# Attention with every score and value matmul on the two 64-row halves of the TensorE array

## The chip, the cores and the metric

The kernel runs on one core of a Trainium2 chip. The metric is device time in microseconds of one execution, the median of several. The profile is of one execution of its own, with times counted from the first instruction.

## The reference

A block of 2048 tokens (width 640) goes through a layer norm without weights, then through attention over a stored cache of keys and values and, beside it, through a gated hidden layer. The two are multiplied and added to the input.

```python
xn = _layernorm(x)                                     # x: 2048 x 640
q = (xn @ wq).reshape(B, Sq, 32, 192)                  # 32 heads, 192 wide
scores = einsum("bhqd,bhkd->bhqk", q, k_cache) * 192 ** -0.5
o = einsum("bhqk,bhkd->bhqd", softmax(scores), v_cache)  # 2048 keys a head
s = o.reshape(B, Sq, 32 * 192) @ wo                    # 6144 -> 640
h = silu(xn @ w1) * (xn @ w3)                          # 640 -> 1536
g = silu(h @ w2)
out = x + s * g
```

All inputs are bf16.

## The kernel before, in words

**Order of work.** After the layer norm of the first 512 tokens the kernel goes head by head (32), and in a head block by block of 512 queries (4, `qb`). Instructions wrapped in `pin` keep the order in which the program writes them on their engine, so the order on TensorE is the order of the Python calls. What is not pinned (some GpSimd copies, loads) is placed by the scheduler.

**Scores, transposed.** Keys lie transposed in SBUF, so that a score tile has 128 keys as rows and 512 queries as columns. The 192 values of a key are split: `KA` holds 128 of them on 128 partitions, `KB` the other 64. A 64-deep matmul fills half of the array's rows. Key tiles are therefore taken in pairs (`p` and `p + 8`, of 16): `KB` holds the last 64 values of the second half of the keys on partitions 64 to 127 and, by a GpSimd copy (line 101), those of the first half on partitions 0 to 63. Query values lie likewise in `qA` (128), `qF` (partitions 64 to 127) and `qD` (a copy on partitions 0 to 63, line 225). For one pair `scores` issues two full matmuls (line 293, into the two 512-column halves of a score tile `st2`) and then two 64-row matmuls, one on each half of the array (line 300), that add to the same places. One ScalarE exponential over 128 x 1024 (line 303) turns the pair into `pT2`, with a bias per head (`nb`) that bounds the scores from above.

**Values.** `pT2` is the stationary operand of the value matmuls (line 323): for both key tiles and each of the block's four tiles of 128 queries, 128 keys deep, with 193 columns. The last column of `vt` is one, so that the sum of the exponentials comes out beside the values. The four query tiles add up in two banks (`obank`, two tiles each) over all 16 key tiles. At the end of a block VectorE takes the reciprocal of the sum (line 339) and multiplies (line 340) into `ostage`, which is stored to DRAM after every second head (line 344).

**Batches.** `advance` takes two or three pairs at once (`uneven`, line 349; `even` with two in head 0): all their full score matmuls, all their 64-row ones, and then the value matmuls of the batch before. In the first batch of a block `between` stands ahead of the values: the projection of the next head's queries (`project_chunk`, lines 219 to 222, ten matmuls with 512 columns, cast by VectorE at lines 223 and 224), and in odd heads a piece of the hidden layer (`swiglu_chunk`) on ScalarE and GpSimd. Half of the columns of `wqB` are hidden-layer weights, so that a part of the hidden layer is projected on the way. VectorE also takes maxima of absolute queries and keys (lines 229 and 237), from which `finish_head` makes `nb`. In head 0 `block_bound` does that for each block, and transposes of the normalised tokens (`next_turn`) and the projections of heads 0 and 1 come between batches.

**Tiles in PSUM.** `ps_st` has three tiles of 1024 f32 (scores, projections, transposes), `ps_o` two of 512: 4096 f32 a partition.

**Loads.** `load_head(h + 2)` is called at the start of head `h`. On SyncE's queue it puts two DMA transposes of 2048 keys by 128 columns (lines 98 and 100) and the load of the values (line 103), and on GpSimd's queue the weights. Three heads of keys fit.

**Tail.** After the last head come 16 hidden-layer chunks (`ffn_hidden`, line 445; the first of them ahead of the last value matmuls), the hidden layer's output (`ffn_out`, line 496) and the product with `wo` (`output_tile`, line 480).

Of the kernel before, what the change touches and what calls it, by code (L numbers as in the profile page):

```python
# [8 lines left out]
ACT = mybir.ActivationFunctionType  # L9
ALU = mybir.AluOpType  # L10
# [19 lines left out]
def _kernel_impl(ctx, tc, A_x, A_k_cache, A_v_cache, A_wq, A_wo, B_w1, B_w3, B_w2, out):  # L30
# [21 lines left out]
    eps = 1e-5  # L52

# [40 lines left out]
    def load_head(h):  # L94
        kh = A_k_cache[0, h]
        vh = A_v_cache[0, h]
        KA = kvp.tile([P, SK], BF16, tag="KA")
        nc.sync.dma_start_transpose(out=KA[:], in_=kh[:, 0:P])
        KB = kvp.tile([P, SK], BF16, tag="KB")
        nc.sync.dma_start_transpose(out=KB[:], in_=kh[:, DH - P:DH])  # L100
        nc.gpsimd.tensor_copy(out=KB[0:DT, 0:HALF], in_=KB[P - DT:P, 0:HALF])
# [12 lines left out]
        return dict(KA=KA, KB=KB, vt=vt, wq=wq, wqB=wqB)  # L114
# [3 lines left out]
    with ExitStack() as actx:  # L118
        qp = actx.enter_context(tc.tile_pool(name="qp", bufs=2))
        pp = actx.enter_context(tc.tile_pool(name="pp", bufs=6))  # L120
        qfp = actx.enter_context(tc.tile_pool(name="qfp", bufs=3))
        lctx = ExitStack()
# [3 lines left out]
        ps_st = pstack.enter_context(tc.tile_pool(name="ps_st", bufs=3, space=bass.MemoryType.PSUM))  # L126
# [75 lines left out]
        def start_head(h):  # L202
            L = loads.pop(h)
            heads[h] = dict(
                h=h, L=L, KA=L["KA"], KB=L["KB"], vt=L["vt"],
                qA=qp.tile([P, SQ], BF16, tag="qA", name="qA"),
                qF=qfp.tile([P, SQ], BF16, tag="qF", name="qF"),
                qD=qp.tile([DT, SQ], BF16, tag="qD", name="qD"),
                st=stt.tile([P, 4, NQB], F32, tag="st", name="st"),
            )  # L210
            pin(nc.vector.memset(heads[h]["st"][0:PGW, :, :], 0.0))

        def project_chunk(h, qb):
            hd = heads[h]
            wq, wqB, KA, KB = hd["L"]["wq"], hd["L"]["wqB"], hd["KA"], hd["KB"]
            qA, qF, qD, st = hd["qA"], hd["qF"], hd["qD"], hd["st"]
# [7 lines left out]
            pin(nc.vector.tensor_copy(out=qF[:, qs], in_=ps[:, 512:1024]))  # L224
            nc.gpsimd.tensor_copy(out=qD[:, qs], in_=qF[PGW:P, qs])  # L225

            def maxima():
                for col, (src, r0) in ((2, (qA, 0)), (3, (qF, PGW))):
                    pin(nc.vector.tensor_reduce(out=st[r0:P, col, qb:qb + 1], in_=src[r0:P, qs], axis=AX.X, op=ALU.max,  # L229
                                                apply_absolute_value=True))  # L230
            return maxima

        def key_maxima(h, cb):
            hd = heads[h]
            cs = slice(cb * 512, (cb + 1) * 512)
            for col, (src, r0) in enumerate(((hd["KA"], 0), (hd["KB"], PGW))):
                pin(nc.vector.tensor_reduce(out=hd["st"][r0:P, col, cb:cb + 1], in_=src[r0:P, cs], axis=AX.X, op=ALU.max,  # L237
                                            apply_absolute_value=True))

        def whole_key_max(col, src, r0):  # L240
            pin(nc.vector.tensor_reduce(out=heads[0]["st"][r0:P, col, 0:1], in_=src[r0:P, :], axis=AX.X, op=ALU.max,
                                        apply_absolute_value=True))

        def block_bound(qb):
            hd = heads[0]
            pr = stt.tile([P, 2], BF16, tag="prb", name="prb")
            pin(nc.vector.scalar_tensor_tensor(out=pr[:], in0=hd["st"][:, 0:2, 0], scalar=-SCALE * SLACK,
                                               in1=hd["st"][:, 2:4, qb], op0=ALU.mult, op1=ALU.mult))
            bp = ps_st.tile([P, 1024], F32, tag="st2", name="bp")
            for t in range(2):  # L250
                pin(nc.tensor.matmul(bp[:, 0:1], lhsT=ones_bf[:], rhs=pr[:, t:t + 1], start=(t == 0), stop=(t == 1)))
            nb = stt.tile([P, 1], F32, tag="nbb", name="nbb")
            pin(nc.vector.tensor_copy(out=nb[:], in_=bp[:, 0:1]))
            hd.setdefault("nb", []).append(nb)

        def finish_head(h):
            hd = heads[h]
            mx = stt.tile([P, 4], F32, tag="mx", name="mx")
            pin(nc.vector.tensor_reduce(out=mx[:], in_=hd["st"][:], axis=AX.X, op=ALU.max))
            pr = stt.tile([P, 2], F32, tag="pr", name="pr")  # L260
            pin(nc.vector.scalar_tensor_tensor(out=pr[:], in0=mx[:, 0:2], scalar=-SCALE * SLACK, in1=mx[:, 2:4],
                                           op0=ALU.mult, op1=ALU.mult))
# [4 lines left out]
            hd["nb"] = [nb] * NQB  # L267
# [15 lines left out]
        def scores(hd, qb, pairs):  # L283
            KA, KB, qA, nb = hd["KA"], hd["KB"], hd["qA"], hd["nb"][qb]
            qt = (hd["qD"], hd["qF"])
            qs = slice(qb * 512, (qb + 1) * 512)
            sts = []
            for p in pairs:
                st2 = ps_st.tile([P, 1024], F32, tag="st2", name="st2")
                sts.append(st2)  # L290
                for t in range(2):
                    kt = p + t * NPAIR
                    pin(nc.tensor.matmul(st2[:, t * 512:(t + 1) * 512], lhsT=KA[:, kt * P:(kt + 1) * P], rhs=qA[:, qs],  # L293
                                     start=True, stop=False))
            pts = []
            for p, st2 in zip(pairs, sts):
                for t in range(2):
                    kt = p + t * NPAIR
                    r = slice(t * DT, (t + 1) * DT)
                    pin(nc.tensor.matmul(st2[:, t * 512:(t + 1) * 512], lhsT=KB[r, kt * P:(kt + 1) * P], rhs=qt[t][r, qs],  # L300
                                     start=False, stop=True))
                pT2 = pp.tile([P, 1024], BF16, tag="pT2", name="pT2")
                pin(nc.scalar.activation(out=pT2[:], in_=st2[:], func=ACT.Exp, scale=SCALE, bias=nb[:]))  # L303
                pts.append(pT2)
            return pts

        def values(batch):
            hd, qb = batch[0][0], batch[0][1]
            h, vt = hd["h"], hd["vt"]
            first, last = batch[0][2] == 0, batch[-1][2] == NPAIR - 1  # L310
            if first:
                acc["o"] = [ps_o.tile([P, 512], F32, tag=f"ob{b}", name=f"obank{b}") for b in range(2)]
            obank = acc["o"]
            hg = h % HG
            if first and hg == 0:
                acc[qb] = stp.tile([P, 4, HG * DH], BF16, tag=f"ostage{qb}", name="ostage")
            ostage = acc[qb]

            def pv(b, p, pT2):
                for t in range(2):  # L320
                    kt = p + t * NPAIR
                    for j in (2 * b, 2 * b + 1):
                        pin(nc.tensor.matmul(obank[b][:, (j % 2) * 256:(j % 2) * 256 + DH + 1],  # L323
                                             lhsT=pT2[:, t * 512 + j * P:t * 512 + (j + 1) * P],
                                             rhs=vt[:, kt, 0:DH + 1],
                                             start=(kt == 0 and j % 2 == 0), stop=(kt == NKT - 1 and j % 2 == 1)))

            if not last:
                for _, _, p, pT2 in batch:
                    for b in range(2):  # L330
                        pv(b, p, pT2)
                return
            for b in range(2):
                for _, _, p, pT2 in batch:
                    pv(b, p, pT2)
                ov = obank[b][:].rearrange("p (j c) -> p j c", j=2)
                i0 = qb * 4 + b * 2
                rl = rl_all[:, h * NQT + i0:h * NQT + i0 + 2]
                pin(nc.vector.reciprocal(out=rl, in_=ov[:, :, DH:DH + 1]))
                pin(nc.vector.tensor_tensor(out=ostage[:, b * 2:b * 2 + 2, hg * DH:(hg + 1) * DH], in0=ov[:, :, 0:DH],  # L340
                                            in1=rl.unsqueeze(2).to_broadcast([P, 2, DH]), op=ALU.mult))
            if hg == HG - 1:
                g0 = h - hg
                acc["store"] = nc.sync.dma_start(
                    out=o_scr[qb].rearrange("(t p) c -> p t c", p=P)[:, :, g0 * DH:(g0 + HG) * DH], in_=ostage[:, :, :])

        assert NPAIR == 8
        even = [[0, 1], [2, 3], [4, 5], [6, 7]]
        uneven = [[0, 1], [2, 3, 4], [5, 6, 7]]
        key_slots = [[0, 1], [2], [3], []]  # L350
        heads = {}
        pend = []

        def advance(hd, qb, pairs, between=None):
            nonlocal pend
            pts = scores(hd, qb, pairs)
            if between:
                between()
            n = len(pairs) if pend else 0
            pend += [(hd, qb, p, pT2) for p, pT2 in zip(pairs, pts)]  # L360
# [295 lines left out]
```

## Time and profile before

| | |
|---|---|
| median of 3 runs | 2045.67 us (2043.2 to 2045.79) |
| the profiled execution | 2045.49 us, its span 2043.6 us |
| granted TensorE clock, mean | 0.996 |
| TensorE busy | 2004.1 us (98%) |
| ScalarE busy | 1152.8 us (56%) |
| VectorE busy | 766.0 us (37%) |
| GpSimd busy | 443.0 us (22%) |
| value matmuls (line 323) | 8192, 35% of the chain that ended last |
| full score matmuls (line 293) | 2048, 21% |
| 64-row score matmuls (line 300) | 2048 in 1024 pairs, 13% |
| projections (lines 220 and 222) | 14% |

PE stands for the matmuls of TensorE, PEld for its loads of the stationary operand, DVE for VectorE, ACT for ScalarE, POOL for GpSimd and SP for SyncE. Matmuls are pipelined: a row's duration runs to its last result and overlaps the next matmul, so a matmul's price is the distance from its start to the next one's start. "Busy" on PE therefore also covers short gaps. Some matmul records are missing from the trace; the counts of loads are complete.

### The profile page before, as it was taken

What the parts mean: (1) busy time and instruction counts of PE and PEld (TensorE: products, weight loads), DVE (VectorE), ACT (ScalarE), POOL (GpSimd) and SP (SyncE); (2) the same over time, 40 slices, a digit from 0 to 9 for tenths busy, and PEclk for the clock granted to TensorE, in tenths of its full rate; (3) what the DMA queues carried; (4) which work ended last, traced back from release to release, by engine and by line L of the source; (5) the groups of instructions that cost most, each with busy time, mean ns of one, the idle gap of its engine ahead of it and who ended that gap; (6) DMA issues with size and microseconds to landing.
All of it is one profiled execution on the core that took longest, in us unless ns stands there. A gap on an engine that the chain in (4) does not pass through costs nothing.

```text
span 2043.6 us, 36569 instructions
## 1 busy us (share of the span) xinstructions
PE 2004.1 (98%) x15480; PEld 1255.9 (61%) x15737; DVE 766.0 (37%) x1584; ACT 1152.8 (56%) x1189; POOL 443.0 (22%) x537
## 2 busy tenths in 40 slices
PE   6999999999999999999999999999999999999998
PEld 3566666666656566656666666666666666567776
DVE  5533444433444334444334443334444331431111
ACT  6666666666666666666666666666666667320000
POOL 2131313130313131312213141313131302000000
PEclk8999999999999999999999999999999999999999
DMA  7122212222222222252423231222132202827882
GB/s 173 41 65 47 66 41 72 51 59 57 64 59 64 59 49 74 43 92 56 118 44 79 44 78 38 63 49 64 42 70 51 58 17 70 242 65 148 148 146 57
DMA packets 350010, 149.37 MB, mean 73 GB/s; under 512 B 301520, under 2 KB 343504, under 8 KB 349840
## 3 DMA queue, kind: packets, MB, share of 16 engines
q1 hardware_dynamic: 337264, 117.98, 26.1%
q0 software_dynamic: 8192, 24.26, 4.8%
q10 hardware_dynamic: 4384, 4.72, 0.9%
q8 instruction: 125, 2.05, 0.4%
q14 instruction: 45, 0.37, 0.1%
HBM read 56.23 MB, written 31.98 MB: 43 GB/s over the span
## 4 chain that ended last, share of the span: by engine, by line
PE 97%; DVE 1%; issue 1%; ACT 1%; DMA 0%; ACTq 0%
PE obank L323 35%; PE st L293 21%; PE st L300 13%; PE ps_s L480 10%; PE ps L220 7%; PE ps L222 7%; PE ps_f L496 3%; PE ps_gu L445 2%; ACT junk L154 0%; ACT pT L303 0%; DVE st L229 0%; DMA x_all<-in_A_x_dram 0%; DVE st L147 0%; PE pst L185 0%; DVE st L237 0%
## 5 line engine op out<-in xcount | busy, mean ns | idle before, releaser
L303 ACT ACTIVATE pT<-st,nb 128x1024 bf16<-128x1024 f32 x992 | 1036.9, 1111 | 576.9 <-PE st L300 576.6
L323 PEld LDWEIGHTS <-pT 128*128 128x128 bf16 x8192 | 673.1, 98 | 143.4 <-issue 112.4
L323 PE MATMUL obank<-vt,pT 128*128 128x193 bf16 x8192 | 750.5, 247 | 0.5 <-DVE ostage L340 0.3
L293 PE MATMUL st<-qA,KA 128*128 128x512 bf16 x1917 | 504.4, 380 | 7.4 <-ACT pT L303 0.5
L223 DVE CAST qA<-ps 128x512 bf16<-128x512 f32 x128 | 88.6, 692 | 972.4 <-PE ps L222 972.4
L293 PEld LDWEIGHTS <-KA 128*128 128x128 bf16 x2048 | 194.6, 98 | 157.5 <-issue 20.9
L300 PE MATMUL st<-qD,KB 64*128 64x512 bf16 x1024 | 288.0, 381 | 0.0
L300 PE MATMUL st<-qF,KB 64*128 64x512 bf16 x1024 | 288.0, 381 | 0.0
L480 PE MATMUL ps_s<-wo_sb,oT 128*128 128x320 bf16 x1536 | 208.8, 299 | 0.0
L300 PEld LDWEIGHTS <-KB 64*128 64x128 bf16 x2048 | 68.3, 94 | 194.5 <-issue 165.1
L480 PEld LDWEIGHTS <-oT 128*128 128x128 bf16 x1536 | 150.3, 98 | 58.3
L225 POOL COPY qD<-qF 64x512 bf16<-64x512 bf16 x128 | 78.3, 611 | 468.7 <-DVE qF L224 460.3
L220 PE MATMUL ps<-xnT,wq 128*128 128x512 bf16 x636 | 161.1, 383 | 1.7 <-ACT xnT L187 1.5
L222 PE MATMUL ps<-xnT,wqB 128*128 128x512 bf16 x522 | 153.9, 381 | 6.2
L340 DVE TENSOR_TENSOR ostage<-obank,rl_all 128x384 bf16<-128x384 f32 x256 | 142.8, 558 | 8.9
L220 PEld LDWEIGHTS <-wq 128*128 128x128 bf16 x640 | 52.7, 98 | 98.4 <-issue 53.4
L222 PEld LDWEIGHTS <-wqB 128*128 128x128 bf16 x640 | 62.9, 98 | 76.3 <-issue 1.4
L277 POOL TENSOR_TENSOR pa<-pt,qF 64x512 bf16<-64x512 bf16 x64 | 72.6, 1144 | 131.9 <-ACT pT L303 117.6
L106 POOL DMA_DIRECT2D wq<-in_A_wq_dram x32 | 32.9, 1027 | 309.0 <-PE ps L220 308.7
L229 DVE TENSOR_REDUCE st<-qF 64x1 f32<-64x512 bf16 x128 | 87.3, 682 | 1.8
L224 DVE CAST qF<-ps 128x512 bf16<-128x512 f32 x128 | 87.1, 680 | 0.0
L229 DVE TENSOR_REDUCE st<-qA 128x1 f32<-128x512 bf16 x128 | 86.5, 676 | 0.0
(68 smaller groups left out, 864.7 us busy)
## 6 DMA issues: line engine op xcount, KB each, us to landing
vt<-in_A_v_cache_dram SPq DMA_DIRECT2D x32, 768.0 KB, 5.2
o_scr<-ostage SPq DMA_DIRECT2D x64, 384.0 KB, 3.6
wo_sb<-in_A_wo_dram POOLq DMA_DIRECT2D x1, 7680.0 KB, 31.4
wq<-in_A_wq_dram POOLq DMA_DIRECT2D x32, 160.0 KB, 3.1
hT_scr<-hblk SPq DMA_DIRECT2D x16, 256.0 KB, 3.3
wqB<-in_B_w_dram POOLq DMA_DIRECT2D x32, 80.0 KB, 2.8
wqB<-in_A_wq_dram POOLq DMA_DIRECT2D x32, 80.0 KB, 2.7
xt<-in_A_x_dram POOLq DMA_DIRECT2D x16, 160.0 KB, 9.3
```

The costliest lines, as they stand in the source:

```text
L220: pin(nc.tensor.matmul(ps[:, 0:512], lhsT=wq[:, c, :], rhs=xnT[:, c, qs], start=(c == 0), stop=(c == DC - 1)))
L222: pin(nc.tensor.matmul(ps[:, 512:1024], lhsT=wqB[:, c, :], rhs=xnT[:, c, qs], start=(c == 0), stop=(c == DC - 1)))
L223: pin(nc.vector.tensor_copy(out=qA[:, qs], in_=ps[:, 0:512]))
L224: pin(nc.vector.tensor_copy(out=qF[:, qs], in_=ps[:, 512:1024]))
L225: nc.gpsimd.tensor_copy(out=qD[:, qs], in_=qF[PGW:P, qs])
L229: pin(nc.vector.tensor_reduce(out=st[r0:P, col, qb:qb + 1], in_=src[r0:P, qs], axis=AX.X, op=ALU.max, apply_absolute_value=True))
L293: pin(nc.tensor.matmul(st2[:, t * 512:(t + 1) * 512], lhsT=KA[:, kt * P:(kt + 1) * P], rhs=qA[:, qs], start=True, stop=False))
L300: pin(nc.tensor.matmul(st2[:, t * 512:(t + 1) * 512], lhsT=KB[r, kt * P:(kt + 1) * P], rhs=qt[t][r, qs], start=False, stop=True))
L303: pin(nc.scalar.activation(out=pT2[:], in_=st2[:], func=ACT.Exp, scale=SCALE, bias=nb[:]))
L323: pin(nc.tensor.matmul(obank[b][:, (j % 2) * 256:(j % 2) * 256 + DH + 1], lhsT=pT2[:, t * 512 + j * P:t * 512 + (j + 1) * P], rhs=vt[:, kt ...
L340: pin(nc.vector.tensor_tensor(out=ostage[:, b * 2:b * 2 + 2, hg * DH:(hg + 1) * DH], in0=ov[:, :, 0:DH], in1=rl.unsqueeze(2).to_broadcast( ...
L480: pin(nc.tensor.matmul(ps, lhsT=oT[:, k, :], rhs=wo_sb[:, k, c0:c1], start=(k == 0), stop=(k == OC - 1)))
```

## The change

**Keys.** `KA`, `KB` and the GpSimd copy go. One tile `KT` of 128 partitions by 3 by 1024 holds, for each of three slots `s`, 64 columns of the first half of the keys on partitions 0 to 63 and 64 columns of the second half on partitions 64 to 127. It is filled by six DMA transposes of 1024 keys by 64 columns. Slot 1 has the chunks the other way round from slot 0 (first half: columns 64 to 127, second half: 0 to 63), and GpSimd makes `qS`, `qA` with its halves swapped (two copies per projection chunk), to go with it.

**Scores.** A pair of key tiles takes three pairs of 64-row matmuls; no full one is left.

**Values.** Each value matmul becomes two, one on keys 0 to 63 of its tile and one on keys 64 to 127. The two halves add up in different banks, so `obank` has four banks (`ps_o`: two tiles of 2 x 512). `evict` copies one half's bank to SBUF (`osum`) and adds the other, and the division reads the sum.

**Score tiles.** `ps_st` goes from three tiles to two: again 4096 f32 a partition. `pT2` goes from six buffers to four.

**Order.** `advance` takes one pair. The value matmuls stand in a list of parts, two per pair (one key tile each; in the last pair of a block one bank pair each). After the scores of a pair parts are issued until three are left, or four where a projection follows. The projection comes after the scores of pair 1; the division of the second bank pair waits (`late`) until the projection is written out. In head 31, where no projection is left, four of the 16 `ffn_hidden` chunks take its place, one in each block, and the tail's remaining chunks use `ps_st` and `ps_o` tiles in turn (`tail_ps`).

**Bounds.** The key maxima are taken per slot; `key_bound` brings the swapped halves together. Head 0's later blocks get their bound by the GpSimd reduction.

The core of the diff:

```diff
-        KA = kvp.tile([P, SK], BF16, tag="KA")
-        nc.sync.dma_start_transpose(out=KA[:], in_=kh[:, 0:P])
-        KB = kvp.tile([P, SK], BF16, tag="KB")
-        nc.sync.dma_start_transpose(out=KB[:], in_=kh[:, DH - P:DH])
-        nc.gpsimd.tensor_copy(out=KB[0:DT, 0:HALF], in_=KB[P - DT:P, 0:HALF])
+        KT = kvp.tile([P, 3, HALF], BF16, tag="KT")
+        for s, chunks in enumerate(((0, 1), (1, 0), (2, 2))):
+            for t, c in enumerate(chunks):
+                nc.sync.dma_start_transpose(out=KT[ROWS[t], s, :],
+                                            in_=kh[t * HALF:(t + 1) * HALF, c * DT:(c + 1) * DT])
...
+            for t in range(2):
+                nc.gpsimd.tensor_copy(out=qS[ROWS[t], qs], in_=qA[ROWS[1 - t], qs])
             nc.gpsimd.tensor_copy(out=qD[:, qs], in_=qF[PGW:P, qs])
...
+            st2 = ps_st.tile([P, 1024], F32, tag="st2", name="st2")
+            for s, qt in enumerate(((hd["qA"],) * 2, (hd["qS"],) * 2, (hd["qD"], hd["qF"]))):
                 for t in range(2):
-                    kt = p + t * NPAIR
-                    pin(nc.tensor.matmul(st2[:, t * 512:(t + 1) * 512], lhsT=KA[:, kt * P:(kt + 1) * P], rhs=qA[:, qs],
-                                     start=True, stop=False))
...
+                    pin(nc.tensor.matmul(st2[:, t * 512:(t + 1) * 512], lhsT=KT[ROWS[t], s, ks], rhs=qt[t][ROWS[t], qs],
+                                         start=(s == 0), stop=(s == 2)))
...
+        def evict(hd, qb, b, ob):
+            ov = ob[:].rearrange("p t (j c) -> p t j c", j=2)
+            osum = osp.tile([P, 2, DH + 1], F32, tag="osum", name="osum")
+            pin(nc.vector.tensor_copy(out=osum[:], in_=ov[:, 0, :, 0:DH + 1]))
+            pin(nc.vector.tensor_tensor(out=osum[:], in0=osum[:], in1=ov[:, 1, :, 0:DH + 1], op=ALU.add))
...
+                    for b in bs:
+                        for j in (2 * b, 2 * b + 1):
+                            for r in range(2):
+                                pin(nc.tensor.matmul(acc["o"][b][:, r, (j % 2) * 256:(j % 2) * 256 + DH + 1],
+                                                     lhsT=pT2[ROWS[r], t * 512 + j * P:t * 512 + (j + 1) * P],
+                                                     rhs=vt[ROWS[r], kt, 0:DH + 1],
...
+        def advance(hd, qb, p, extra=None):
+            pT2 = scores(hd, qb, p)
+            parts.extend(values(hd, qb, p, pT2))
+            while len(parts) > (4 if extra else 3):
+                parts.pop(0)()
+            if extra:
+                extra()
+            while late:
+                late.pop(0)()
...
+                for p in range(NPAIR):
+                    advance(hd, qb, p, extra if p == 1 else None)
```

## The prediction

> **What bounds the kernel now.** I read the page's busy times first, then the costliest groups, then the timeline of one query block in the middle, because a busy PE is not a PE at its peak.
>
> ```profile
> span 2043.6 us, 36569 instructions
> PE 2004.1 (98%) x15480; PEld 1255.9 (61%) x15737; DVE 766.0 (37%) x1584; ACT 1152.8 (56%) x1189; POOL 443.0 (22%) x537
> PE 97%; DVE 1%; issue 1%; ACT 1%; DMA 0%; ACTq 0%
> L323 PE MATMUL obank<-vt,pT 128*128 128x193 bf16 x8192 | 750.5, 247 | 0.5 <-DVE ostage L340 0.3
> L300 PE MATMUL st<-qD,KB 64*128 64x512 bf16 x1024 | 288.0, 381 | 0.0
> L300 PE MATMUL st<-qF,KB 64*128 64x512 bf16 x1024 | 288.0, 381 | 0.0
> ```
>
> PE is 97% of the chain that ended last, and almost nothing makes it wait. Only fewer or better spaced matmuls can help. The timeline shows their spacing (start, duration, what; a group's duration holds the 0.16 us by which the last result comes after its slot):
>
> ```profile
> 1004.59 1.24 PE L222 MATMUL ps<-xnT,wqB 128*128 128x512 bf16 x4
> 1005.67 1.50 PE L323 MATMUL obank<-vt,pT 128*128 128x193 bf16 x16
> 1007.00 1.46 PE L293 MATMUL st<-qA,KA 128*128 128x512 bf16 x6
> 1008.40 0.39 PE L300 MATMUL st<-qD,KB 64*128 64x512 bf16 x1
> 1008.40 0.39 PE L300 MATMUL st<-qF,KB 64*128 64x512 bf16 x1
> 1008.62 0.38 PE L300 MATMUL st<-qD,KB 64*128 64x512 bf16 x1
> 1008.63 0.38 PE L300 MATMUL st<-qF,KB 64*128 64x512 bf16 x1
> 1008.84 0.38 PE L300 MATMUL st<-qD,KB 64*128 64x512 bf16 x1
> 1008.84 0.38 PE L300 MATMUL st<-qF,KB 64*128 64x512 bf16 x1
> 1009.15 2.17 PE L323 MATMUL obank<-vt,pT 128*128 128x193 bf16 x24
> 1011.16 1.49 PE L293 MATMUL st<-qA,KA 128*128 128x512 bf16 x5
> ```
>
> Five projections from 1004.59 to 1005.67 (one record is missing) are 0.216 us each, 16 value matmuls from there to 1007.00 are 0.0833 us each. Neither border between full-array groups costs anything. Two 64-row matmuls on different halves start together, and the next pair 0.216 us later: a pair costs what one full matmul costs. But the batch from 1007.00 to 1011.16 takes 4.16 us, while 6 x 0.216 + 3 x 0.216 + 24 x 0.0833 is 3.94. The 0.22 us lie at the two borders between full-array and 64-row work, some 0.106 us each (from start to start, 0.311 us instead of 0.216 at the border and some 0.011 more on the next matmul).
>
> A whole block takes 13.35 us (1002.00 to 1015.35 in the same view): 34 slots of 0.2158 (16 KA, 8 KB pairs, 10 projections) and 64 of 0.0833 make 12.67; six borders make 0.64; 0.04 is left for a wait. **The borders are the only slack in a block**: 5%.
>
> **The change, part by part.** *Borders.* Scores and values now both run on halves, so only the projection leaves that mode: two borders per block. Heads 1 to 31 have 124 blocks: 124 x 4 x 0.106 = 52.6 us less. Head 31 has no projection, but gets a hidden-layer chunk in its place, with two borders. Head 0 had 16 batches, 32 borders; now 13 turns and projections cut in, 26 borders: 0.6 less. The first hidden chunk behind the last block adds two, 0.2. Together -53.0.
>
> *Scores.* Per pair of key tiles two full matmuls and one pair of halves (3 slots) become three pairs of halves (3 slots). The rows above price a pair at 0.216, so 0; its two starts lie 0.003 apart, which three pairs could lose: 1024 x 0.009 = 9 us at most, 0 taken since the next pair comes at 0.216.
>
> *Values, the term that decides.* 8192 matmuls of 193 columns become 8192 pairs. No row shows such a pair. From below, 0.0833, if a pair costs one full matmul as with 512 columns: 0. From above, two in turn, 0.167: +682 us. Nearest is the L300 pair, the same two halves, so I take 0. But it moves 512 columns; here four instructions (two loads, two matmuls) must be supplied in 0.083 us, 0.021 each, and over a pair of key tiles 44 in 1.31 us, 0.030 each. The trace shows 0.003 between the members of a pair, and 0.055 per load and matmul, 0.027 per instruction, in a short run of transposes:
>
> ```profile
> 34.67 0.63 PEld L185 LDWEIGHTS <-xn 128*128 128x128 bf16 x10
> 34.75 0.72 PE L185 MATMUL pst<-ident_bf,xn 128*128 128x128 bf16 x10
> ```
>
> Its longest dense stretch, head 31 from 1640 to 1741 us (826 matmuls, 837 loads by the windows), needs only 0.061 per instruction. So a steady supply below 0.030 is unproven. The break-even is near: 53 us over 8192 pairs is 6.5 ns, a pair of 0.090 us.
>
> The Trainium skill, "TensorE: Matmul & The Clock Gate", section "Back-to-back issue gap", speaks against the change: in a stream of loads and matmuls it gives about 81 ns per matmul of 128 columns, some 40 ns per instruction. The transposes above, at 55 ns, disagree, though only over ten; by that rule the 372 instructions of a block (186 matmuls with their loads) would take an estimated 15.1 us, and the kernel about 2260 us.
>
> *Eviction.* Per half-block a copy and an addition of 128x386 join the division on DVE. The nearest row is the 128x384 multiply (L340, 0.558); ends are the 128x2 reciprocal (0.160) and the 128x512 cast (0.692). At 0.56 each, DVE goes from 5.2 us (windows, a block of head 19) to about 7.4 of 12.9. I laid the block out from its first score matmul: scores 0 to 0.65, two value parts of 0.33 to 1.31 (the second ends bank pair 0), scores to 1.96, the part that ends bank pair 1 to 2.29, projection 2.40 to 4.56, scores 4.66 to 5.31, then the first values of the new block. DVE has both bank pairs copied and added by about 4.5: 0.8 us before those values. The projection's casts start 0.036 after its last result (1005.87 in the timeline) and take 1.29, to 6.05; the score tile that waits for them comes at 6.31. Cover 0.2 to 0.3 us: 0. If it fails, the two score matmul buffers (three before) make PE wait; one DVE multiply and reciprocal slipping ahead (0.72) costs 0.5 us a block, +60. From below, the present 0.04 us wait may go: -5.
>
> *ACT.* A block holds eight exponentials in 8.36 us (windows), now of 12.9. A value part starts 1.65 us after its scores end; the result lag (0.2) and the exponential (1.11) take 1.31. Cover 0.33 us: 0.
>
> *POOL.* Two qS copies more per chunk (0.61 each, L225): 156 us, less 33 for the KB copies that go. 443 becomes 566 us of 2000. The copies stand behind weight-load issues and ahead of the bound's reduction; what they make is wanted one block or more later: 0.
>
> *Queues.* SP issues six key transposes per head, not two (2.24 and 2.64 us of SP by L98 and L100). Of half the rows and half the columns, six cost 6.7 us if they scale and 15.8 if not, against 4.9; vt and the stores queue behind them. A head lasts 51 us and its keys are loaded a head ahead: 0. At the start nothing hides it. Scores began at 25.07, after two key maxima of 2.28 that ended at 24.73. Now three of about 1.22 (between 0.69 for 512 and 2.28 for 2048 columns) and four small operations of 0.16 would end at 24.6; but if each transpose takes 2.6 of SP after the first (14.07), the last keys land near 29 and scores start at 31. Ends -0.5 and +6; 2 taken, nearer to the scaling, as 4096 packets took 7 us there and 6144 come now.
>
> *Tail.* The same matmuls, in alternating buffers; there PE is busy 88.8 of 89 us already: 0.
>
> **Sum**, against the profiled execution's 2045.49 us (0.2 below the median): 2045.5 - 53.0 + 2 = 1994.5, so 1995. Its own range: 1985 (-5, -2.5, and 2 less for head 0's stalls) to 2040 (half the slip of eviction, scores +9, start +4).
>
> **Rivals.** *A pair of value matmuls costs more than one* (slower). Place: the 16384 half matmuls with their loads. It decides from 0.090 us a pair on. Against it: the L300 pairs. For it: nothing in the trace runs so dense. At the transposes' 27 ns per instruction, unevened by the slower scores, a pair takes 0.108: 8192 x 0.0247 = +202 us, 1995 + 202 = 2197; midway, at 0.096, about 2100. Chance 0.24, of which 0.02 within 0.2% of before.
>
> *Two score buffers are too few* (still faster). The slip above in every block: 1995 + 124 x 0.3 to 0.4 = 2030 to 2045. The order of the casts and the slack of 0.2 us speak against, ACT at 65% too. Chance 0.13, of which 0.02 at or beyond the break-even.
>
> *The borders are not of the mode*, and scores to values keep their 0.1 us: about 2050 with the start. Against it: values to KA and projection to values cross without a gap in the same lines. Chance 0.03.
>
> *As forecast*: 0.60.
>
> **Chances.** Measurement tells 0.2% (4 us) from no change. Faster: 0.60 + 0.11 = 0.71; same: 0.02 + 0.01 = 0.03; slower: 0.22 + 0.01 + 0.03 = 0.26. The range, 1984 to 2150, takes in the slow buffers and the milder half of the dear pairs, and leaves out some 0.15.
>
> **What would show it.** Right: after, a block near 12.9 us; value pairs that start 3 to 4 ns apart, the next 0.083 later; the gap of 0.31 only on both sides of the projection; DVE near 7.4 a block. Wrong: value pairs spaced over 0.090 with PEld "issue" idle growing; PE waiting for DVE casts at the score matmuls; scores starting after 29.

## The result, and the profile after

The changed kernel takes **16609.16 us** (16589.02 to 16642.77), the kernel before 2045.73 us beside it: 8.123 times as long, with an interval of 8.108 to 8.138. The forecast was 1995 us, with a range up to 2150. It is wrong in sign and by a factor of eight, and none of the rivals was this one.

The page of the changed kernel: span, busy time, granted clock and DMA share in 40 slices, packets, the chain that ended last by engine and by line, and two rows of the DMA issues (count, KB each, median us from issue to landing).

```profile
span 16587.2 us, 58267 instructions
PE 2182.7 (13%) x25971; PEld 1440.9 (9%) x25971; DVE 1023.5 (6%) x2131; ACT 1220.6 (7%) x1189; POOL 605.7 (4%) x764
...
PEclk5555555555555555555555555555555555555559
DMA  9999999999999999999999999999999999999995
...
DMA packets 12802963, 142.37 MB, mean 9 GB/s; under 512 B 12754384, under 2 KB 12796368, under 8 KB 12802704
...
SPq 98%; PE 2%; issue 0%; DVE 0%; DMA 0%; ACT 0%; DVEq 0%
SPq L101 81%; SPq L104 16%; PE ps_s L510 1%; SPq L329 1%; PE ps_f L526 0%; SPq L296 0%; PE obank L348 0%; PE st L305 0%; PE ps_gu L427 0%; DMA o_scr<-ostage 0%; DVE a L432 0%; DVE hT L433 0%; ACT t L430 0%; SPq L141 0%; PE ps L223 0%
...
KT<-in_A_k_cache_dram SPq DMA_DIRECT2D x192, 128.0 KB, 168.9
vt<-in_A_v_cache_dram SPq DMA_DIRECT2D x32, 768.0 KB, 89.7
```

Four things are to be seen. PE's 97% of the chain has become SP's 98%: 81% of the span is SP at line 101, the key loads, and 16% at line 104, the value load that stands behind them in the queue. The DMA engines are busy all the time and move 9 GB/s. There are 12.8 million packets, nearly all under 512 bytes. And the key loads are called `DMA_DIRECT2D`, a plain copy, although the line calls `dma_start_transpose`. Before, the key rows of the same view read:

```profile
DMA packets 350010, 149.37 MB, mean 73 GB/s; under 512 B 301520, under 2 KB 343504, under 8 KB 349840
...
KA<-in_A_k_cache_dram SPq DMA_TRANSPOSE x32, 5.2
KB<-in_A_k_cache_dram SPq DMA_TRANSPOSE x32, 4.9
```

The packets tell what the copy does. SP's queue had 337,264 before and has 12,790,128 now, 12.45 million more. The 192 loads of 64 columns by 1024 keys hold 12,582,912 values, and the trace holds exactly as many packets of two bytes, where the kernel before has none. The 64 wide transposes that went had 131,072 packets of 256 bytes, 2048 each. So each value of two bytes is a packet of its own. Over the span this is 16587 us / 12.79 million = 1.30 ns a packet, all engines together.

The timeline of SP's queue (start, duration, line, operation) gives the pace of the whole kernel:

```profile
3.37 421.04 SPq L101 DMA_DIRECT2D KT<-in_A_k_cache_dram  x6
424.44 81.44 SPq L104 DMA_DIRECT2D vt<-in_A_v_cache_dram  x1
505.93 427.41 SPq L101 DMA_DIRECT2D KT<-in_A_k_cache_dram  x6
```

The six key loads of a head hold SP for 411 to 439 us (median 420), and its value load, queued behind them, for 81. Before, a head's two key transposes held SP for 2.24 and 2.64 us (medians). Counted from the first exponential of one head to that of the next, a head takes 471 to 537 us, against 53.4 before. Everything else in the kernel waits for that.

### The profile page after: what moved, and what is told of

It reads as the page before. It is cut to its first block, busy times and chain, and to the rows that moved or that the text cites. A ratio compares the mean times of both kernels' runs of the same rounds, so it can differ in the third digit from the quotient of the medians.

```text
span 16587.2 us, 58267 instructions
## 1 busy us (share of the span) xinstructions
PE 2182.7 (13%) x25971; PEld 1440.9 (9%) x25971; DVE 1023.5 (6%) x2131; ACT 1220.6 (7%) x1189; POOL 605.7 (4%) x764
## 3 DMA queue, kind: packets, MB, share of 16 engines
q1 hardware_dynamic: 12790128, 109.60, 180.9%
## 4 chain that ended last, share of the span: by engine, by line
SPq 98%; PE 2%; issue 0%; DVE 0%; DMA 0%; ACT 0%; DVEq 0%
SPq L101 81%; SPq L104 16%; PE ps_s L510 1%; SPq L329 1%; PE ps_f L526 0%; SPq L296 0%; PE obank L348 0%; PE st L305 0%; PE ps_gu L427 0%; DMA o_scr<-ostage 0%; DVE a L432 0%; DVE hT L433 0%; ACT t L430 0%; SPq L141 0%; PE ps L223 0%
## 5 line engine op out<-in xcount | busy, mean ns | idle before, releaser
L348 PE MATMUL obank<-vt,pT 64*128 64x193 bf16 x16384 | 987.3, 259 | 13337.1 <-DVE osum L319 13128.8
L348 PEld LDWEIGHTS <-pT 64*128 64x128 bf16 x16384 | 814.8, 100 | 13610.2 <-DVE osum L319 11321.8
L325 DVE TENSOR_TENSOR ostage<-osum,rl_all 128x384 bf16<-128x384 f32 x256 | 145.7, 569 | 11327.6 <-DMA o_scr<-ostage 11319.8
L229 POOL COPY qS<-qA 64x512 bf16<-64x512 bf16 x256 | 186.1, 727 | 14666.1 <-DVE qA L226 14657.7
L305 PE MATMUL st<-qA,KT 64*128 64x512 bf16 x2048 | 442.7, 406 | 483.1 <-DVE qF L227 452.6
L305 PE MATMUL st<-qS,KT 64*128 64x512 bf16 x2048 | 442.2, 405 | 35.1 <-issue 35.1
L305 PE MATMUL st<-qF,KT 64*128 64x512 bf16 x1024 | 412.8, 403 | 4.1 <-issue 4.1
L305 PE MATMUL st<-qD,KT 64*128 64x512 bf16 x1024 | 412.4, 403 | 2.5 <-issue 2.5
L305 PEld LDWEIGHTS <-KT 64*128 64x128 bf16 x6144 | 328.9, 100 | 730.1 <-issue 629.9
L319 DVE TENSOR_TENSOR osum<-osum,obank 128x386 f32<-128x386 f32 x256 | 142.6, 557 | 8.9
## 6 DMA issues: line engine op xcount, KB each, us to landing
vt<-in_A_v_cache_dram SPq DMA_DIRECT2D x32, 768.0 KB, 89.7
```

Source lines behind the costliest of these rows:

```text
L229: nc.gpsimd.tensor_copy(out=qS[ROWS[t], qs], in_=qA[ROWS[1 - t], qs])
L305: pin(nc.tensor.matmul(st2[:, t * 512:(t + 1) * 512], lhsT=KT[ROWS[t], s, ks], rhs=qt[t][ROWS[t], qs], start=(s == 0), stop=(s == 2)))
L348: pin(nc.tensor.matmul(acc["o"][b][:, r, (j % 2) * 256:(j % 2) * 256 + DH + 1], lhsT=pT2[ROWS[r], t * 512 + j * P:t * 512 + (j + 1) * P], ...
```

## Experiments

All kernels here start from the changed one unless it is said otherwise, and each is compared with the kernel before on its own chip (2044.8 to 2045.4 us in these runs). Head times are from a head's first exponential to the next head's first one. From head 1 on they are given apart for odd and even heads, because the swiglu of a pair of heads runs in the odd ones.

### The same matmuls with wide key loads

The 64-column loads go, and the two wide transposes of the kernel before come back. GpSimd makes the two halves that the slots need beside them:

```diff
-        KT = kvp.tile([P, 3, HALF], BF16, tag="KT")
-        for s, chunks in enumerate(((0, 1), (1, 0), (2, 2))):
-            for t, c in enumerate(chunks):
-                nc.sync.dma_start_transpose(out=KT[ROWS[t], s, :], ...)
+        nc.sync.dma_start_transpose(out=KA[:], in_=kh[:, 0:P])
+        nc.sync.dma_start_transpose(out=KB[:], in_=kh[:, DH - P:DH])
+        nc.gpsimd.tensor_copy(out=KA[DT:P, 0:HALF], in_=KA[0:DT, HALF:SK])
+        nc.gpsimd.tensor_copy(out=KB[0:DT, HALF:SK], in_=KB[DT:P, 0:HALF])
```

Two pools (`osp`, `lnp`) go from two buffers to one for the space, and the key maxima are eight small ones a head instead of six.

> The changed kernel, with its keys loaded as before, by two transposes of 128 columns, and the swapped halves made by two GpSimd copies of 64x1024; all 20480 half matmuls of the attention stay. Theory (the 64-column loads are the whole loss, the matmul side of the forecast holds): 1995 us, between 1985 and 2040, a block near 12.9 us, the gap of 0.31 us only on both sides of the projection. Rival (the half matmuls or the two score buffers lose as well): 2046 us or more, with value pairs above 0.090 us apart or PE waiting for DVE.

Measured: **2021.08 us** (2020.47 to 2022.88), 0.9882 of before (0.9866 to 0.9899). From the page and the DMA issues:

```profile
span 2019.0 us, 58336 instructions
PE 1958.2 (97%) x25836; PEld 1307.2 (65%) x25971; DVE 1103.1 (55%) x2226; ACT 1222.1 (61%) x1189; POOL 668.5 (33%) x828
...
DMA packets 350099, 150.76 MB, mean 75 GB/s; under 512 B 301520, under 2 KB 343504, under 8 KB 349840
...
KA<-in_A_k_cache_dram SPq DMA_TRANSPOSE x32, 5.2
KB<-in_A_k_cache_dram SPq DMA_TRANSPOSE x32, 5.1
```

The form of the key loads is thus the whole loss of 14.6 ms; the rest of the change, with the two copies that replace the narrow loads, makes the kernel 1.2% faster. But 1995 is not reached either. The span is 26 us over the forecast's, and the head times say where: the first exponential starts at 30.0 us (28.5 before, 30.5 forecast), head 0 takes 70.7 (67.1 before, 66.5 forecast), odd heads take 53.23 and even ones 51.27 (53.4 before, 51.70 forecast), and the stretch from head 31 on takes 350.7 (346.1 before, 344.6 forecast). The odd heads are 1.5 us above the forecast. The even ones are slightly under it, partly because they begin late and catch up, as is seen below.

### The kernel before with its 128 columns loaded as twice 64

The reverse, to measure the load alone, in the kernel before:

```diff
-        nc.sync.dma_start_transpose(out=KA[:], in_=kh[:, 0:P])
+        for r in range(2):
+            nc.sync.dma_start_transpose(out=KA[r * DT:(r + 1) * DT, :], in_=kh[:, r * DT:(r + 1) * DT])
```

> The kernel before, with KA alone loaded by two transposes of 64 columns. Theory (such a load is no transpose but one packet for every 2-byte element, and the packets bound everything): 32 x 2048 x 128 = 8.39 million packets; the changed kernel had 12.79 million in 16587 us, 1.30 ns each, so some 8.7 million in all and 11200 us. Rival (a fixed price for each DMA of this kind: the changed kernel had 192 at a median of 81.5 us of SP): 64 of them, 5200 us plus what is left, under 7300 us.

Measured: **12043.78 us**, one run, nearer to the theory's 11200 than to the rival's 7300. Queue 1 and the key rows of the DMA issues:

```profile
q1 hardware_dynamic: 8660336, 117.98, 172.6%
...
KA<-in_A_k_cache_dram SPq DMA_DIRECT2D x64, 256.0 KB, 265.7
...
KB<-in_A_k_cache_dram SPq DMA_TRANSPOSE x32, 169.8
```

The same 117.98 MB as before now take 8,660,336 packets: 8,323,072 more, which is 64 loads of 64 x 2048 values (8,388,608 packets of two bytes in the trace) less 32 wide transposes of 2048 packets. Over the time of the kernel before, the kernel loses 9999 us, 1.20 ns per added packet; the changed kernel loses 14,588 us against the one with wide keys, 1.17 ns per added packet. A price per load would give a third of that loss here (64 narrow loads against 192); it gives 69%, as the packets do (67%). `KB`, still a transpose, lands after 169.8 us instead of 4.9, as it queues behind the copies; the value load, now behind `KB`, lands after 6.6 us.

### Values on the full array

With wide keys, the values alone go back to one matmul of 128 rows into one bank, without the addition. Scores stay on halves, so each pair of key tiles now crosses twice between full-array and 64-row work, 16 borders a block:

```diff
-                            for r in range(2):
-                                pin(nc.tensor.matmul(acc["o"][b][:, r, ...], lhsT=pT2[ROWS[r], ...], rhs=vt[ROWS[r], kt, 0:DH + 1], ...))
+                            pin(nc.tensor.matmul(acc["o"][b][:, 0, ...], lhsT=pT2[:, ...], rhs=vt[:, kt, 0:DH + 1], ...))
```

> As wide_keys, but the value matmuls run on the full array again (one bank of each pair, no addition), so that every pair of key tiles crosses from half to full and back: 16 borders a block, not 2. Theory (0.106 us for every border between the two modes): wide_keys + 124 x 14 x 0.106 + 38 x 0.106 for head 0 = wide_keys + 188 us. Rival (the gap belongs to the KB matmuls or to their score tile, not to the mode): within 10 us of wide_keys.

Measured: **2181.58 us**, 1.0667 of before (1.0649 to 1.0684), 160.5 us over the kernel with wide keys. The timeline of PE, first with wide keys, then with full values (start, duration, what):

```profile
1156.31 0.91 PE L352 MATMUL obank<-vt,pT 64*128 64x193 bf16 x16
...
1158.36 0.38 PE L309 MATMUL st<-qA,KA 64*128 64x512 bf16 x2
1158.58 0.38 PE L309 MATMUL st<-qS,KB 64*128 64x512 bf16 x1
...
1158.80 0.38 PE L309 MATMUL st<-qF,KB 64*128 64x512 bf16 x1
1159.01 0.83 PE L352 MATMUL obank<-vt,pT 64*128 64x193 bf16 x16
1159.68 0.38 PE L309 MATMUL st<-qA,KA 64*128 64x512 bf16 x2
```

```profile
1190.17 0.39 PE L309 MATMUL st<-qA,KA 64*128 64x512 bf16 x2
...
1190.61 0.38 PE L309 MATMUL st<-qD,KB 64*128 64x512 bf16 x1
...
1190.92 0.84 PE L350 MATMUL obank<-vt,pT 128*128 128x193 bf16 x8
1191.70 0.39 PE L309 MATMUL st<-qA,KA 64*128 64x512 bf16 x2
```

With wide keys, a pair of key tiles takes 1159.68 - 1158.36 = 1.32 us; eight pairs of value matmuls take 1159.68 - 1159.01 = 0.67, that is 0.083 each, the price of a full value matmul. With full values it takes 1.53, with a gap of 0.31 from the last scores to the first value. 3 x 0.216 + 8 x 0.0833 is 1.31, so the two borders cost 0.21, 0.105 each. Both terms that the forecast had staked most on are confirmed: the border's 0.106 us and the value pair's 0.0833. Of the 188 us that 14 more borders a block would make, 27 are missing. Some 21 of them are missing in heads 1 to 30, where the slower PE hides a loss of the odd heads that the next section is about: odd heads take 57.56 us here and even ones 57.42. The rest is missing in head 0, which is no longer than with wide keys, and from head 31 on. Against an undisturbed even head of the last kernel below, 51.58 us, a head takes 5.9 us more, and 56 borders of 0.105 are 5.9.

### The bound's order on GpSimd

What do odd heads lose? The timeline of GpSimd with wide keys, at the end of odd head 21, with ScalarE's first exponential behind it:

```profile
1191.41 1.29 POOL L230 COPY qS<-qA 64x512 bf16<-64x512 bf16 x2
1192.75 0.61 POOL L231 COPY qD<-qF 64x512 bf16<-64x512 bf16 x1
1199.42 0.40 POOL L274 PARTITION_ALL_REDUCE nb<-ns  x1 [6.06 <-issue]
```

```profile
1197.13 1.11 ACT L312 ACTIVATE pT<-st,nb 128x1024 bf16<-128x1024 f32 x1 [0.20 <-PE st L309]
1199.86 2.12 ACT L312 ACTIVATE pT<-st,nb 128x1024 bf16<-128x1024 f32 x2 [1.62 <-POOL nb L274]
```

Ahead of the reduction that makes the bound `nb`, GpSimd waits 6.06 us for nothing that the profile shows. In the built program an instruction of GpSimd without a row of its own stands there, `PseudoReloadLibraryIndex`. It names library 1 ahead of a reduction that follows operations of another kind (the swiglu's), and library 0 ahead of such operations when they follow a reduction, and once at the start. The wait is called the reload here. In even heads the same gap is 1.1 us and belongs to VectorE. In the kernel before, the reload was there too (99.2 us of it in 16 places), but the bound was ready about 1.6 us early. Now two copies stand ahead of it, and ScalarE waits for `nb` 22.0 us in all, 5.2 of it in head 0.

The first attempt to mend it wrote the last chunk's copies behind the reduction (the expectations call the copies into `qS` and `qD` q.scale and q.diff):

```diff
-            for t in range(2):
-                nc.gpsimd.tensor_copy(out=qS[ROWS[t], qs], in_=qA[ROWS[1 - t], qs])
-            nc.gpsimd.tensor_copy(out=qD[:, qs], in_=qF[PGW:P, qs])
...
+                if bound_first:
+                    bound_first()
+                    copies()
```

> The kernel with the wide key loads (2021.1 us), with the q.scale and q.diff copies of a head's last chunk issued on GpSimd behind the bound's reduction and not ahead of it. Theory (the copies and the reload of some 6 us that follows the swiglu's use of GpSimd make the bound late in odd heads): ScalarE's waits on nb outside head 0, 16.8 us, go; odd heads come from 52.5-53.3 us to about 51.5, the kernel to 2004-2007 us. Rival (the odd heads lose their time to the tanh of the projection on ScalarE, wherever the bound stands): within 3 us of 2021, and the wait on nb is replaced by one on ScalarE's own work.

A second kernel has, besides, one reduction early in head 0 whose result nobody uses, and the tail's gate matmuls in the other pair of banks:

```diff
+        nc.gpsimd.tensor_copy(out=warm[:, 0:1], in_=heads[0]["qS"][:, 0:1])
+        nc.gpsimd.partition_all_reduce(warm[:, 1:2], warm[:, 0:1], P, bass_isa.ReduceOp.add)
...
-            return ps_o.tile([P, 2, 512], F32, tag=f"ob{turn[0] // 2 % 2}", ...)
+            return ps_o.tile([P, 2, 512], F32, tag=f"ob{(turn[0] // 2 + 1) % 2}", ...)
```

> As the kernel with the early bound, and besides: one reduction of GpSimd whose result nobody uses, issued at the start ahead of the second pair of heads' loads, and the tail's gate matmuls put into the other pair of the four banks. Theory (what GpSimd spends ahead of its first reduction, and what the tail waits for the last addition, stand on the path): the 5.2 us wait on nb in head 0 goes and 1 to 2 us of the 2.2 us ahead of the tail's first matmul, together 1998-2001 us. Rival (the start is set by the loads of keys and the tail by its own chain): within 1 us of the kernel with the early bound.

Measured: **2032.68 us** (0.9928 of before; 0.9915 to 0.9942) and **2028.17 us** (0.9919; 0.9905 to 0.9932), both slower than wide keys alone. Neither theory nor rival gave this, for the edit did not change what it was meant to change. GpSimd at the end of head 17 in the first of the two, and then in the kernel with wide keys:

```profile
985.74 1.29 POOL L231 COPY qS<-qA 64x512 bf16<-64x512 bf16 x2
987.09 0.61 POOL L232 COPY qD<-qF 64x512 bf16<-64x512 bf16 x1
987.64 1.04 POOL L82 DMA_DIRECT2D w_sb<-in_B_w_dram  x1
998.06 0.40 POOL L281 PARTITION_ALL_REDUCE nb<-ns  x1 [9.37 <-issue]
```

```profile
983.37 0.61 POOL L231 COPY qD<-qF 64x512 bf16<-64x512 bf16 x1
989.85 0.40 POOL L274 PARTITION_ALL_REDUCE nb<-ns  x1 [5.87 <-issue]
990.13 1.21 POOL L82 DMA_DIRECT2D w_sb<-in_B_w_dram  x1
```

The copies are not pinned, and the scheduler put them ahead of the reduction as before. What did move is a 1.9 MB weight load, from behind the reduction to ahead of it, and there the reload took 9.37 us instead of 5.87. Heads 15, 17 and 18, around the weight loads, are together 8.4 us longer than with wide keys alone. So this pair of runs does not decide between theory and rival. Its side results stand: head 0 takes 69.9 us instead of 70.7 with the early reduction, its 5.2 us wait for `nb` gone, and the stretch from head 31 on takes 347.3 us instead of 350.7, since the first gate matmul behind the last block waits 0.16 us for VectorE's addition and not 2.21.

### The reload moved instead of the copies

Now the reload is moved: a reduction that nobody uses stands behind the last swiglu chunk of each pair of heads.

```diff
             if qb == NQB - 1:
                 nc.sync.dma_start(out=hT_scr[m * PGW:(m + 1) * PGW, :], in_=hblk[:, :])
+                reload(hblk[:, SQ - 1:SQ], PGW)
...
+        def reload(after, n):
+            nc.gpsimd.tensor_copy(out=warm[0:n, 0:1], in_=after)
+            nc.gpsimd.partition_all_reduce(warm[:, 1:2], warm[:, 0:1], P, bass_isa.ReduceOp.add)
```

> The kernel with the wide key loads (2021.1 us), with a reduction of GpSimd whose result nobody uses behind the last chunk of each swiglu, so that the reload of some 6 us comes there, some 25 us before the bound is wanted; the q.scale and q.diff copies stay ahead of the bound. Theory (the reload in front of the bound is what the odd heads lose): the waits for the bound outside head 0, 16.8 us, go; the 15 odd heads, 52.4 to 53.7 us from exp to exp, come to about 51.6, and the kernel to 2000-2005 us. Rival (the odd heads lose it to the swiglu's own work, tanh on ScalarE or what GpSimd takes from VectorE): odd heads stay over 52.4, the kernel within 5 us of 2021.

A second kernel adds the two side results, the reduction in head 0 and the other banks in the tail.

> As the kernel with the early reload, and the two additions that the run with the reduction at the start and the other pair of banks in the tail had: head 0 took 0.8 us less there than with the wide key loads alone, the stretch from the last head on 3.5 us less. Theory (these are waits on the path, independent of the odd heads): 4 to 5 us below the kernel with the early reload, 1996-2001 us, which is the forecast of 1995 but for the start. Rival (what is saved in head 0 and in the tail was given by the later odd heads' disorder): within 1 us of the kernel with the early reload.

Measured: **2015.08 us** (0.9855 of before; 0.984 to 0.987) and **2010.5 us** (0.9837; 0.9823 to 0.985). The first of them keeps one wait of ScalarE for `nb`, 5.5 us in head 0, the second none. Odd heads fall from 53.23 to 52.13 us, even ones rise from 51.27 to 51.58, because an even head no longer begins late and catches up. Heads 1 to 30 take 1555.7 us, 11.8 less. The reload was the larger part of the odd heads' loss; some 0.5 us of each remains, as the rival has it, and the trace of the last kernel below shows where. The additions are worth 4.6 us together, as expected. Yet both kernels are some 10 us above what was expected, and part of that lies at a place that nobody had named: the first exponential starts at 34.4 and 35.0 us, not 30.0. The start of GpSimd with wide keys, and then with the moved reload:

```profile
2.69 0.30 POOL masks.py:199 TENSOR_SCALAR_AFFINE_SELECT ident_bf<-ident_bf 128x128 bf16<-128x128 bf16 x1 [0.35 <-issue]
```

```profile
14.08 0.28 POOL masks.py:199 TENSOR_SCALAR_AFFINE_SELECT ident_bf<-ident_bf 128x128 bf16<-128x128 bf16 x1 [11.77 <-issue]
```

GpSimd's program is the same up to there, a reload of library 0 ahead of the select included. But one program ends with the swiglu's operations on GpSimd (library 0), the other with a reduction (library 1).

### The last unused reduction left out

```diff
-                reload(hblk[:, SQ - 1:SQ], PGW)
+                if m < H // 2 - 1:
+                    reload(hblk[:, SQ - 1:SQ], PGW)
```

> As the kernel with all three additions, but without the unused reduction behind the last swiglu (head 31), so that GpSimd ends an execution as it did in the kernel with the wide key loads. Theory (the 11 us in front of the identity's select at the start are a reload that an execution owes to what the one ahead of it left in GpSimd): the first exp comes at 30.0-30.6 us and not at 35.0, head for head nothing else changes, the kernel at 2003-2006 us against 2010.5. Rival (the start is late because the program has more of such reloads, wherever they stand): first exp at 34-35, within 1 us of 2010.5.

Measured: **2004.72 us** (2004.01 to 2006.57), 0.9804 of before (0.9791 to 0.9818), the fastest of all. GpSimd at the start, and at the end of odd head 21:

```profile
2.68 0.30 POOL masks.py:199 TENSOR_SCALAR_AFFINE_SELECT ident_bf<-ident_bf 128x128 bf16<-128x128 bf16 x1 [0.35 <-issue]
```

```profile
1174.45 0.40 POOL L308 PARTITION_ALL_REDUCE warm<-warm  x1 [6.12 <-issue]
...
1183.11 0.61 POOL L234 COPY qD<-qF 64x512 bf16<-64x512 bf16 x1
1184.84 0.38 POOL L277 PARTITION_ALL_REDUCE nb<-ns  x1 [1.11 <-DVE st L218]
```

The select is back at 2.68 us and the first exponential at 30.9; heads 1 to 30 take 1553.9 us. The theory holds: the late start comes and goes with the last reduction. That what one execution leaves in GpSimd is paid by the next is concluded from this; a profile shows one execution only. The reload now stands 10 us ahead of the bound (25 had been expected), and the bound waits 1.11 us as in even heads.

What is left in the odd heads can be read from this trace. The division at the end of a half block (line 338, `osum` into `ostage`) in a block of even head 20, and then in one of odd head 21, with GpSimd's swiglu beside it, the projection's second cast and the score matmul that waits for it:

```profile
1099.84 0.56 DVE L338 TENSOR_TENSOR ostage<-osum,rl_all 128x384 bf16<-128x384 f32 x1
```

```profile
1150.34 2.26 POOL L298 TENSOR_TENSOR pa<-pt,qF 64x512 bf16<-64x512 bf16 x2 [6.96 <-issue]
1151.46 1.56 DVE L338 TENSOR_TENSOR ostage<-osum,rl_all 128x384 bf16<-128x384 f32 x1
...
1154.79 0.68 DVE L231 CAST qF<-ps 128x512 bf16<-128x512 f32 x1
...
1155.53 0.39 PE L318 MATMUL st<-qA,KA 64*128 64x512 bf16 x2 [0.19 <-DVE qF L231]
```

The division takes 0.56 us in 127 of the 128 places where no `TENSOR_TENSOR` or copy of GpSimd runs beside it, and over 0.6 us in 38 of the 47 where a `TENSOR_TENSOR` does. In the kernel before it takes 0.56 us in all 256 places, 30 of them beside such an operation; there it reads the values from PSUM (`obank`), here from SBUF (`osum`). In 11 of the 15 odd heads the first division of one block takes 1.37 to 1.56 us. Just these blocks last 13.4 to 13.8 us, all others of heads 1 to 30 at most 13.2. So the rest of the odd heads' loss, some 6.6 us in all, goes with what GpSimd takes from VectorE, the second half of the rival above. It comes with the new eviction. No run takes this overlap away.

## Why the prediction was wrong

**The step that failed is "Queues"**: "six cost 6.7 us if they scale and 15.8 if not, against 4.9 ... A head lasts 51 us and its keys are loaded a head ahead: 0." Six loads hold SP for 420 us (median), 27 times the upper end, and no head can hide that. Both ends were worked out from the rows of the 128-column transposes, on the assumption that the call with 64 columns is the same operation on less data. It is another operation, named so in the profile after and already in the built program: the key loads of the changed kernel are plain copies there, those before are transposes. The working even used the right unit, the packet count, but counted 6144 packets for the six loads where 393,216 came.

The Trainium skill warns of it: "DMA: Bandwidth & Descriptors", section "DMA Transpose (X-bar)", under its constraints, says that for a DRAM input smaller than one tile of the transpose, with fewer than 128 elements in the free dimension, software can fall back to a rearranged access pattern with inefficient descriptors. The runs agree (64 columns: a copy by values; 128: a transpose), and put the price beside it: 1.17 to 1.20 ns a value, 8.1 times the kernel's time. The prediction did not draw on that sentence.

**Borders**: right. 0.105 us each with full values against 0.106, and the even heads of the last kernel, 51.58 us, are 0.1 under the 51.70 of the forecast: a block of 12.90 us, as predicted.

**Values**: right, and with it the rival of dear pairs is refuted: 0.083 us a pair, where 0.090 was the break-even. A pair of key tiles with its 44 loads and matmuls takes 1.32 us in the lines above, 30 ns an instruction. By the rule of the Trainium skill that was weighed ("TensorE: Matmul & The Clock Gate", "Back-to-back issue gap", about 81 ns per matmul of 128 columns with its load, so an estimated 40 ns an instruction) a block would take an estimated 15.1 us; this case's traces disagree with the rule carried over like this.

**Scores, ACT**: right at 0. Three pairs of halves start 0.22 us apart in the timeline. The rival of borders that are not of the mode falls: with wide keys scores and values follow each other without a gap.

**Eviction**: right at 0 in the even heads, where VectorE works 7.4 to 8.2 us in a block (heads 20 and 22 of the last kernel; 7.4 predicted) and blocks take 12.9 us. In the odd heads the 0 fails: "At 0.56 each" left out that the division now reads SBUF, and beside GpSimd's swiglu it takes up to 1.56 us. That is more than the 0.2 to 0.3 us of cover, and the block loses 0.5 to 0.9 us. So the rival of too few score buffers is refuted for the other blocks, but what it describes, PE waiting for VectorE, shows in one block of 11 odd heads.

**POOL**: wrong, though hidden behind the keys in the changed kernel. "Ahead of the bound's reduction; what they make is wanted one block or more later: 0" followed the consumer of the copies and forgot the bound queued behind them, which had 1.6 us to spare ahead of a 6 us reload. Taking the reload out of there is worth 11.8 us over heads 1 to 30; the 15 odd heads had lost 1.5 us each against the forecast.

**Start and tail**: the start moved by 1.5 us with wide keys (2 taken for the narrow ones, which in fact take 515.5 us to the first exponential). The tail's 0 was 2.2 us short at the change of banks.

With the keys wide and these waits removed the sum nearly closes. The last kernel's span of 2002.2 us is 9.6 above the 1992.6 that the forecast makes of the span before: start 0.4, head 0 3.4, heads 1 to 30 2.9 and the rest 2.8. What is still missing in head 0 and behind head 31 was not followed further.

## What to carry to other kernels

When a change gives an operation a smaller shape, do not scale its price: look up in the built program whether it is still the same operation, and count its packets before its bytes. Price an added instruction also by what is queued behind it on its engine, not only by who reads its result. Where an operand moves from PSUM to SBUF, look at what the other engines do while it is read. And read a new order of work from the trace before judging what the order is worth: one edit here moved a weight load and left the copies where they were.

## What the runs showed of the hardware

- A transposing load of 64 columns of two-byte values ran as a copy with one packet per value: 1.17 to 1.20 ns per added packet, against 2048 packets and some 5 us for a transpose of 2048 keys by 128 columns. What stands directly behind it on the queue suffers too: the 768 KB value load landed after 89.7 us instead of 5.2. Where a wide transpose stood between (the second run), the transpose landed after 169.8 us and the value load after 6.6.
- In the changed kernel, where PE mostly waits, the granted clock was 0.566 in the mean, and the matmuls were busy for 2182.7 us against 1958.2 with wide keys. Where the granted clock was 0.5, pairs of 64-row score matmuls started 0.427 us apart, and where it was 1, 0.216 us.
- GpSimd took about 6 us ahead of a partition reduction that follows the swiglu's operations, 9.4 us where a 1.9 MB load had just been issued, and 11 to 12 us at the start, beside the first loads, in the two programs that end with a reduction.
- A VectorE multiply of 128x384 f32 with its input in SBUF took 0.56 us alone and up to 1.56 us beside GpSimd's tensor operations; with its input in PSUM it took 0.56 us beside them too.
